# A recurrent state kept as diagonal blocks only, and one unit's transposes of r issued one addition later

## The chip, the cores and the metric

The kernel runs on one core of one Trainium2 chip. The metric is the device time of one execution in microseconds (us), lower is better. Every execution has such a time; a profiled one has, besides, a span from its first to its last instruction and a record of each instruction. The engines are called as in the profile: PE is TensorE (PEld its weight loads), DVE is VectorE, ACT is ScalarE, POOL is GpSimd, and SP is SyncE, which here issues the DMAs.

## What is computed

A linear attention with a decaying state (RWKV-6) is followed by a two-layer network with a SiLU between the layers. All is float32, with B = 4 batches, H = 8 heads, S = 768 time steps and D = 48 channels per head. The state of each batch and head is a 48x48 matrix, and in the reference it moves one step of time at a time:

```python
state = np.zeros((B, H, D, D))
for t in range(S):
    kt, vt, rt, wt = (k[:, :, t], v[:, :, t], r[:, :, t], w[:, :, t])
    cur = np.einsum('bhd,bhe->bhde', u[None] * kt, vt)
    y[:, :, t] = np.einsum('bhd,bhde->bhe', rt, state + cur)
    state = wt[:, :, :, None] * state + np.einsum('bhd,bhe->bhde', kt, vt)
x = y.transpose(0, 2, 1, 3).reshape(B * S, H * D)        # 3072 x 384
h = x @ w_in                                             # 384 x 2048
out = (h / (1 + np.exp(-h))) @ w_out                     # 2048 x 384
```

## The kernel before, in words

**Units.** Time is cut into six chunks of L = 128 steps, and the four batches into two pairs. That gives twelve units, numbered i = 0 to 11, with chunk n = i // 2. Units of one pair follow each other at a distance of two and hand on the state of that pair.

**Heads in pairs.** Eight heads of 48 channels lie as NP = 4 pairs p. The even head of a pair is in partitions 0 to 47 (e = 0), the odd one in partitions 64 to 111 (e = 1); PD = 64 is that distance. The state tile (line 289) holds for each batch and pair 128 columns: the even head's block stands in its rows at columns 0 to 47, the odd head's in its rows at columns 64 to 111. The two blocks are the diagonal of a 128x128 square, and the rest of it stays zero after `clear_state` (line 404).

**One unit.** The tokens of w, k and r come by DMA in 32x32 blocks (`load_blocks`) and are put channels-first by `turn` (line 374), two VectorE transposes of 128x512 for each of the three, one per batch. In the first two units `turn` uses TensorE instead. The products of w over 2, 4, ... 128 steps are made level by level on POOL (`product`, line 422). Keys are multiplied by them on POOL (`start_keys` at line 669, `grow_keys` at 645, `grow_own` at 654), and queries on VectorE (`grow_queries` at 627, `prepare` at 779). `burst` lets TensorE make the scores of two levels at once (line 703); `keep_level` puts them into the score tile. Then `y_state` (line 843) multiplies r by the state that the unit found, `y_values` (line 864) the scores by the values, and `update` makes the state for the pair's next unit: products k by v on TensorE (line 892), the old state times the decay of the whole chunk on POOL (line 897), and the sum of both on VectorE (line 906). `update` has the middle step only in chunks 1 to 4, that is in units 2 to 9, once per batch; the last chunk has no update.

**The network.** For each unit, `up` (line 1000) makes the hidden layer in eight steps, with the SiLU on ACT (line 1009). `quarter` (line 1066) makes the output in seven products of half-size blocks, in the manner of Strassen, from sums of the operands that VectorE makes beforehand (`sums`, line 1048; `weight_sums`, line 1040). The products take turns in two PSUM banks named p_o. Product 0's bank is emptied by a copy on ACT (line 1073), every later one's by one or two additions on VectorE (line 1075). So product 2 waits for the copy after product 0, and product 3 for the addition after product 1, which is the second.

**The order of work.** The order is written out by hand, and each engine executes its own instructions in that order. For unit 3 and later, `mix(i)` returns groups of steps of the scan, and the main loop puts steps of the network between them: the products of the output of unit i - 2 (`downs`), then the hidden layer of unit i - 1 (`ups`).

```python
for group, count in zip(groups, room):
    do(*group)
    for step in steps[:count]:
        do(*step)
    steps = steps[count:]
```

`room` for unit 3 begins 1, 1, 0, 2: after its first group comes product 0, after its second product 1, after its third nothing, after its fourth products 2 and 3. Unit 3 is the only one below NPAIR = 4 that goes through `mix`; later units have other groups, in which the turns of w and k are issued at the end of the unit before, behind `y_values`, and `update` comes after them; the turns of r and the first step of `grow_own` (lines 654 and 627) make the first group, and products 0 and 1 both follow it (their `room` begins 2, 1, 2, 2), so that the addition after product 1 stands behind them on VectorE.

**Queues.** Nearly all DMAs are issued by SP in the order of the program. A transpose on VectorE waits first for the DMA semaphores of its blocks.

Of the kernel before, what the change touches and what calls it, by code (L numbers as in the profile page):

```python
# [8 lines left out]
F32 = mybir.dt.float32  # L9
# [29 lines left out]
def kernel(  # L39
# [11 lines left out]
    nc = tc.nc  # L51

    B, H, S, D = r.shape
    DM, DF = moe_w_in.shape
    L = 128
    NL = 7
    NB = 2
    NP = H // 2
    PD = 64
# [14 lines left out]
    const = ctx.enter_context(tc.tile_pool(name="const", bufs=1))  # L74
# [9 lines left out]
    def bank(name, *dims):  # L84

        have = banks[name][turns_of[name] % 2][:]
        turns_of[name] += 1
        steps, n = [], 1
        for d in dims[::-1]:
            steps.insert(0, [n, d])  # L90
            n *= d
        return bass.AP(tensor=have.tensor, offset=have.offset, ap=[have.ap[0], *steps])
# [193 lines left out]
    make_identity(nc, ident)  # L286


    state = const.tile([128, B, NP, 2 * PD], F32, name="state")

    room = pt.tile([128, 4, DM // 2], F32, name="partial", bufs=1).rearrange("p x d -> p (x d)")
    spread = room[:, 0:4 * L].rearrange("p (s b t) -> p s b t", s=2, b=NB)
# [65 lines left out]
    tw, tr, tk, diag, kq, xt = {}, {}, {}, {}, {}, {}  # L358
# [472 lines left out]
    def values(i, b):  # L831
        return vq[i] if b == 1 else vt[i]

    def y_state(i):

        n, b0 = units[i]
        for e in range(2):
            p_yt[i, e] = bank("p_m", NP, L)
        for p in range(NP):
            for b in range(NB):  # L840
                for e in range(2):
                    rows = slice(PD * e, PD * e + D)
                    nc.tensor.matmul(y_place(i, e, p, b), lhsT=state[rows, b0 + b, p, rows],  # L843
                                     rhs=tr[i][rows, b * NP + p, :], start=(p < 2 and b == 0), stop=False)

        half = L // 2
        for p in range(NP):
            for b in range(NB):
                rows, at = slice(b * half, (b + 1) * half), (2 * p + b) * D
                nc.tensor.matmul(y_place(i, b, p, b)[:, 0:half], lhsT=whole[i][b][rows, at:at + D],  # L850
                                 rhs=score[rows, i % NSC, b, b * NP + p, 0:half], start=False, stop=False)

    def y_place(i, e, p, b):

        x = p % 2
        return p_yt[i, e][PD * x:PD * x + D, p // 2 * NB + b, :]
# [27 lines left out]
    def update(i, b):  # L884
        n, b0 = units[i]
        if n == S // L - 1:
            return
        if b == 0:
            p_kv[i] = bank("p_m" if i < NTOK else "p_sc", NB, NP, D)
        for p in range(NP):  # L890
            for e in range(2):
                nc.tensor.matmul(p_kv[i][PD * e:PD * e + D, b, p, :], lhsT=kq[i, b][:, p, PD * e:PD * e + D],
                                 rhs=values(i, b)[:, 2 * p + e, :], start=(b == 0 and p == 0),
                                 stop=(b == NB - 1 and p == NP - 1))
        new = state[:, b0 + b]
        if n > 0:
            nc.gpsimd.tensor_tensor(out=new, in0=new,
                                    in1=tw[i][NL][:, b * NP:(b + 1) * NP, :].to_broadcast([128, NP, 2 * PD]),
                                    op=ALU.mult)
        if b < NB - 1:  # L900
            return
        for e in range(2):
            rows, cols = slice(PD * e, PD * e + D), slice(PD * e, PD * e + D)
            new = state[rows, b0:b0 + NB, :, cols]
            if n > 0:
                nc.vector.tensor_tensor(out=new, in0=p_kv[i][rows], in1=new, op=ALU.add)
            else:
                (nc.scalar.copy if i == 0 else nc.vector.tensor_copy)(out=new, in_=p_kv[i][rows])
# [23 lines left out]
    def both(fn, i, *args):  # L932
        return [(fn, i, b, *args) for b in range(NB)]

    def block_loads(i, names="wkr"):
        return [(load_blocks, i, name, g) for name in names for g in range(4)]

    def mix(i):

        ahead = i + 1 < len(units)  # L940

        def at(now, *steps):
            return steps if now else ()

        def bonus_steps(j, *steps):
            return [(block_bonus, j, x) for x in steps]

        def sum_steps(j, *steps):
            return [(block_sum, j, x) for x in steps]

        def turns(j):
            return [*both(turn, j, "w"), (product, j, 0), *both(turn, j, "k")]

        def start(j):
            return [*[(product, j, l) for l in range(1, NL)], (grow_own, j, 1)]

        end = [[*at(ahead, *bonus_steps(i + 1, 0, 1, 2, 3))],
               [*at(i < len(units) - NB, (turn_apart, i), (turn_k, i)), (y_state, i), *both(y_values, i), *at(ahead, *turns(i + 1)),
                (sums, i - 1, FH // 2 - 2), *both(update, i), *at(not ahead, (move_x, i))]]
        if i < NPAIR:  # L960
            groups = [[*both(turn, i, "w"), (product, i, 0)],
                      [*both(turn, i, "k"), *both(turn, i, "r"), (odd_ones, i)], [(start_levels, i), (prepare_keys, i, 1)],
                      [(prepare, i, 1), *[(product, i, l) for l in range(1, NL)]],
                      [(burst, i, 1), (keep_level, i, 1)],
                      [(keep_level, i, 2), (go_on, i, 2)],
                      [(prepare, i, 3), (reverse_v, i), (bonus, i, 0)],
                      [(burst, i, 3), (keep_level, i, 3), (bonus_sum, i, 0), (bonus, i, 1), (bonus, i, 2)],
                      [(keep_level, i, 4), (go_on, i, 4), (bonus_sum, i, 1), (load_rk, i + 1), (load_u,)],
                      [(prepare, i, 5), (make_block_mask,), (bonus_spread, i), (bonus_write, i)],
                      [(burst, i, 5), (keep_level, i, 5), (keep_level, i, 6), (go_on, i, 6)], *end]  # L970
        else:
            groups = [[*both(turn, i, "r"), (grow_own, i, 0)], [*start(i), *sum_steps(i, 0, 1), *bonus_steps(i, 4, 5), (move_x, i - 1)],
                      [(odd_keys, i, 2), (grow_keys, i, 2, False), (grow_queries, i, 2), *sum_steps(i, 2)],
                      [(prepare, i, 3), *bonus_steps(i, 6, 7)],
                      [(burst, i, 3), (keep_level, i, 3), *sum_steps(i, 3, 4), (block_move, i), *at(ahead, (load_rk, i + 1))],
                      [(keep_level, i, 4), (go_on, i, 4)],
                      [(prepare, i, 5), (reverse_v, i)],
                      [(block_spread, i), (block_write, i)],
                      [(burst, i, 5), (keep_level, i, 5), (keep_level, i, 6), (go_on, i, 6)], *end]

        loads = [*at(i >= NPAIR and ahead, *block_loads(i + 1, "r")), *at(i + NSLOT < len(units), *block_loads(i + NSLOT, "wk"))]
        if i + 1 < len(units):
            loads.insert(len(loads) // 2, (load_values, i + 1))

        behind = groups[10 if i < NPAIR else 5 if i == NPAIR else 2:][:4 if i + NSLOT >= len(units) else None]
        for at, group in enumerate(behind):
            group += loads[at * len(loads) // len(behind):(at + 1) * len(loads) // len(behind)]
        return groups
# [127 lines left out]
    for l in range(1, NL):  # L1116
# [9 lines left out]


    others = {1: [(bonus_sum, 1, 0), (bonus_sum, 1, 1), (load_rk, 2), *blocks[8:12]], 2: [*both(update, 0)],
              3: [(bonus_spread, 1), (reverse_v, 1), (clear, 1), (load_values, 2)]}

# [19 lines left out]
    for m in range(6):  # L1150
# [8 lines left out]
    do((burst, 2, 5), (keep_level, 2, 5), (keep_level, 2, 6), (go_on, 2, 6), (bonus_write, 2), (up, 1, 6), (weight_sums, 1),  # L1159
       (load_values, 3), (turn_apart, 2), (turn_k, 2), (up, 1, 7), (weight_sums, 2), (sums, 1, 2))  # L1160
    do((sums, 1, 3), (y_state, 2), *both(y_values, 2), *both(update, 2),
       (move_x, 2),
       *blocks[7:])

    for i in range(3, len(units)):
        steps = downs(i - 2) + ups(i - 1)
        groups = mix(i)
        if i == NTOK + 1:
            groups[4].insert(1, (weight_sums, 3))
        room = (1, 1, 0, 2, 1, 1, 1, 1, 1, 2, 2, 1, 1) if i < NPAIR else (2, 1, 2, 2, 1, 1, 1, 2, 1, 1, 1)  # L1170
# [5 lines that stand above are left out]
# [32 lines left out]
```

## Time and profile before

| | |
|---|---|
| median of three runs | 605.8 us (603.47, 605.80, 605.83) |
| time of the profiled execution | 599.81 us |
| its span, first to last instruction | 598.0 us |
| busy: PE, PEld | 588.5, 528.1 us |
| busy: VectorE, POOL, ACT | 418.0, 363.3, 233.1 us |
| granted TensorE clock | 1.000 |
| moved by DMA | 53.42 MB, mean 89 GB/s |

A line of a group of instructions names the line of the kernel, the engine, the operation, the tile written and the tiles read, and the shapes (partitions x elements). For one tile's instructions the page gives the count, then the shortest, median and longest duration in ns and the first and last start. A line of the timeline begins with the start and the length in us, and merges neighbours of one form (x2); a bracket at its end gives how long the engine sat idle before and what released it. A line of the waits has the total in us, how often, and the longest. "Releasers" are inferred from semaphore events.

### The profile page before, as it was taken

What the parts mean: (1) busy time and instruction counts of PE and PEld (TensorE: products, weight loads), DVE (VectorE), ACT (ScalarE), POOL (GpSimd) and SP (SyncE); (2) the same over time, 40 slices, a digit from 0 to 9 for tenths busy, and PEclk for the clock granted to TensorE, in tenths of its full rate; (3) what the DMA queues carried; (4) which work ended last, traced back from release to release, by engine and by line L of the source; (5) the groups of instructions that cost most, each with busy time, mean ns of one, the idle gap of its engine ahead of it and who ended that gap; (6) DMA issues with size and microseconds to landing.
All of it is one profiled execution on the core that took longest, in us unless ns stands there. A gap on an engine that the chain in (4) does not pass through costs nothing.

```text
span 598.0 us, 14761 instructions
## 1 busy us (share of the span) xinstructions
PE 588.5 (98%) x5790; PEld 528.1 (88%) x5790; DVE 418.0 (70%) x709; ACT 233.1 (39%) x516; POOL 363.3 (61%) x414
## 2 busy tenths in 40 slices
PE   8999999999999999999999999999999999999997
PEld 7787876799899899898899899889889889889997
DVE  7879788798696695596696697687588587542041
ACT  6788884431530530440351361361351251250110
POOL 6998778247678668388578577577567667500000
PEclk9999999999999999999999999999999999999999
DMA  9956893443541543643643643643553531101000
GB/s 224 297 129 198 166 285 46 61 75 49 128 63 57 109 65 55 136 62 53 135 61 55 135 61 52 132 61 51 104 90 51 120 60 27 36 1 28 28 0 27
DMA packets 203078, 53.42 MB, mean 89 GB/s; under 512 B 186752, under 2 KB 194816, under 8 KB 203008
## 3 DMA queue, kind: packets, MB, share of 16 engines
q1 hardware_dynamic: 201424, 51.88, 42.6%
q8 instruction: 46, 0.75, 0.5%
q10 hardware_dynamic: 1584, 0.59, 0.5%
q14 instruction: 24, 0.20, 0.1%
HBM read 43.21 MB, written 5.24 MB: 81 GB/s over the span
## 4 chain that ended last, share of the span: by engine, by line
PE 77%; DVE 5%; DMA 5%; SPq 5%; POOL 3%; ACT 2%; issue 2%; DVEq 0%; POOLq 0%; ACTq 0%
PE p_h L1000 33%; PE p_o L1066 31%; SPq L123 3%; PE p_m L1022 3%; PE p_sc L703 2%; PE p_m L864 2%; PE p_m L843 2%; PE p_m L703 1%; DMA raw<-in_r_dram 1%; DMA tokens_rk<-in_k_dram 1%; DVE score L721 1%; DMA tokens_w<-in_w_dram 1%; POOL w_out_sb L255 1%; PE p_sc L819 1%; POOL tk L645 1%
## 5 line engine op out<-in xcount | busy, mean ns | idle before, releaser
L1000 PE MATMUL p_h<-xt,w_in_sb 128*128 128x256 f32 x1152 | 259.4, 382 | 0.9 <-POOL tk L669 0.7
L1000 PEld LDWEIGHTS p_h<-xt,w_in_sb 128*128 128x128 f32 x1152 | 215.7, 190 | 31.9 <-POOL tk L669 0.9
L1009 ACT ACTIVATE gt<-p_h 128x512 f32<-128x512 f32 x90 | 53.6, 596 | 171.4 <-PE p_h L1000 171.0
L645 POOL TENSOR_TENSOR tk<-tk,tw 128x256 f32<-128x256 f32 x128 | 93.6, 752 | 33.6 <-issue 20.7
L1066 PE MATMUL p_o<-own,temps 128*128 128x192 f32 x528 | 88.7, 327 | 1.6 <-DVE temps L1075 1.6
L507 POOL TENSOR_TENSOR ruk<-tokens_rk 128x768 f32<-128x768 f32 (+1 forms) x32 | 53.8, 1691 | 57.2 <-DMA tokens_rk<-in_k_dram 37.2
L1066 PEld LDWEIGHTS p_o<-own,temps 128*128 128x128 f32 x528 | 86.0, 190 | 2.6 <-DVE temps L1075 2.5
L1066 PE MATMUL p_o<-w_out_sb,gt 128*128 128x192 f32 x508 | 86.6, 327 | 0.0
L1066 PEld LDWEIGHTS p_o<-w_out_sb,gt 128*128 128x128 f32 x508 | 83.3, 190 | 1.0 <-DVE partial L1075 0.4
L1048 DVE TENSOR_TENSOR temps<-gt 128x256 f32<-128x256 f32 x84 | 53.2, 633 | 25.6 <-ACT gt L1009 25.3
L627 DVE TENSOR_TENSOR tr<-tr,tw 128x512 f32<-128x512 f32 x61 | 57.5, 942 | 16.0 <-PE p_m L703 12.5
L422 POOL TENSOR_TENSOR tw<-tw 128x256 f32<-128x256 f32 (+6 forms) x83 | 41.0, 494 | 36.4 <-DVE tw L374 32.5
L615 ACT COPY tk<-tk 128x256 f32<-128x256 f32 x52 | 20.9, 403 | 106.9 <-POOL tk L645 76.9
L721 DVE COPY_PREDICATED score<-mask,p_sc 128x512 f32<-128x512 int8 x42 | 31.2, 798 | 3.9 <-PE p_sc L703 3.7
L1048 DVE TENSOR_TENSOR temps<-temps,gt 128x256 f32<-128x256 f32 x43 | 32.3, 751 | 1.5
L1066 PE MATMUL p_o<-w_out_sb,temps 128*128 128x192 f32 x176 | 30.4, 326 | 0.0
L541 DVE TENSOR_REDUCE block_sums<-ruk 128x4 f32<-128x192 f32 (+1 forms) x48 | 24.2, 545 | 7.1 <-POOL ruk L507 7.1
L1066 PEld LDWEIGHTS p_o<-w_out_sb,temps 128*128 128x128 f32 x176 | 28.9, 190 | 0.0
L1075 DVE TENSOR_TENSOR temps<-p_o,partial 128x192 f32<-128x192 f32 x22 | 7.9, 358 | 29.8 <-PE p_o L1066 23.5
L869 ACT COPY yt<-p_m 48x512 f32<-48x512 f32 x40 | 23.2, 581 | 13.8 <-PE p_m L864 13.1
L1075 DVE TENSOR_TENSOR partial<-p_o,partial 128x192 f32<-128x192 f32 x33 | 11.7, 354 | 23.6 <-PE p_o L1066 23.6
L654 POOL TENSOR_TENSOR tk<-tk,tw 128x256 f32<-128x256 f32 x32 | 27.6, 883 | 0.0
(188 smaller groups left out, 811.2 us busy)
## 6 DMA issues: line engine op xcount, KB each, us to landing
w_out_sb<-in_moe_w_in_dram SPq DMA_DIRECT2D x6, 768.0 KB, 7.2
w_out_sb<-in_moe_w_out_dram SPq DMA_DIRECT2D x4, 768.0 KB, 6.3
own<-in_moe_w_out_dram SPq DMA_DIRECT2D x4, 768.0 KB, 5.7
tokens_rk<-in_r_dram SPq DMA_DIRECT2D x8, 384.0 KB, 4.3
tokens_rk<-in_k_dram SPq DMA_DIRECT2D x8, 384.0 KB, 5.3
tokens_w<-in_w_dram SPq DMA_DIRECT2D x8, 384.0 KB, 6.3
xt<-yt SPq DMA_DIRECT2D x60, 48.0 KB, 1.9
raw<-in_w_dram SPq DMA_DIRECT2D x80, 32.0 KB, 2.1
```

Of the source, the lines that this page charges most:

```text
L422: engine.tensor_tensor(out=up, in0=t[:, :, 0::2], in1=t[:, :, 1::2], op=ALU.mult)
L507: mul = lambda out, one, two: nc.gpsimd.tensor_tensor(out=out, in0=one, in1=two, op=ALU.mult)
L541: add = lambda out, have: nc.vector.tensor_reduce(out=out, in_=have, axis=mybir.AxisListType.X, op=ALU.add)
L627: nc.vector.tensor_tensor(out=odd, in0=odd, in1=tw[i][l][:, :, 0::2][:, :, :, None].to_broadcast([128, Q, L >> (l + 1), c]), op=ALU.mult)
L645: nc.gpsimd.tensor_tensor(out=out, in0=have, in1=odd_products(i, l, b, *blocks), op=ALU.mult)
L654: nc.gpsimd.tensor_tensor(out=have, in0=have, in1=odd_products(i, l, b, [2, NP * ni]), op=ALU.mult)
L721: nc.vector.copy_predicated(out=dst, mask=masks[l][:, :, None].to_broadcast([128, NB, NP, ni, c]), data=sc[e].rearrange("p (b q) (i c) -> ...
L869: nc.scalar.copy(out=yt[i][PD * e:PD * e + D, x::2, :, :], in_=p_yt[i, e][PD * x:PD * x + D].rearrange("p (q b) t -> p q b t", b=NB))
L1000: nc.tensor.matmul(p_h[:, a, :], lhsT=w_in_sb[:, c, f * 128:(f + 1) * 128], rhs=xt[i][:, c, :], start=(c == 0), stop=(c == KC - 1))
L1009: nc.scalar.activation(out=gt[i, m], in_=p_h, func=AF.Silu)
L1048: nc.vector.tensor_tensor(out=out, in0=one, in1=two, op=op)
L1066: nc.tensor.matmul(p, lhsT=left(f), rhs=right[:, f, :], start=(f == 0), stop=(f == FH - 1))
```

## The change

The state tile loses the columns that were always zero: each batch and pair now has 48 columns, and both heads' blocks start at column 0, each in its own partitions. `y_state`, the product with the decay and the sum in `update` use the new columns. In the groups of unit 3, the turns of r leave the second group, where they stood behind the turns of k, and become the first steps of the third. Between these two groups lies product 1 with its addition.

```diff
-    state = const.tile([128, B, NP, 2 * PD], F32, name="state")
+    state = const.tile([128, B, NP, D], F32, name="state")
...
-                    nc.tensor.matmul(y_place(i, e, p, b), lhsT=state[rows, b0 + b, p, rows],
+                    nc.tensor.matmul(y_place(i, e, p, b), lhsT=state[rows, b0 + b, p, :],
                                      rhs=tr[i][rows, b * NP + p, :], start=(p < 2 and b == 0), stop=False)
...
             nc.gpsimd.tensor_tensor(out=new, in0=new,
-                                    in1=tw[i][NL][:, b * NP:(b + 1) * NP, :].to_broadcast([128, NP, 2 * PD]),
+                                    in1=tw[i][NL][:, b * NP:(b + 1) * NP, :].to_broadcast([128, NP, D]),
                                     op=ALU.mult)
...
-            rows, cols = slice(PD * e, PD * e + D), slice(PD * e, PD * e + D)
-            new = state[rows, b0:b0 + NB, :, cols]
+            rows = slice(PD * e, PD * e + D)
+            new = state[rows, b0:b0 + NB]
...
             groups = [[*both(turn, i, "w"), (product, i, 0)],
-                      [*both(turn, i, "k"), *both(turn, i, "r"), (odd_ones, i)], [(start_levels, i), (prepare_keys, i, 1)],
+                      [*both(turn, i, "k"), (odd_ones, i)], [*both(turn, i, "r"), (start_levels, i), (prepare_keys, i, 1)],
```

## The prediction

> **What bounds the kernel now.** I read the page first (busy shares), then TensorE's waits in order of length, then the state tile's own instructions, and last the order of time around the waits.
>
> ```profile
> PE 588.5 (98%) x5790; PEld 528.1 (88%) x5790; DVE 418.0 (70%) x709; ACT 233.1 (39%) x516; POOL 363.3 (61%) x414
> ```
>
> TensorE (PE) is busy for all but 9.5 us of 598.0. The table by stretches puts 3.1 us of those before 36 us and 1.6 us between 36 and 121.5 us, where nothing of the change but one memset lies. After that 4.8 remain, in which the waits over 0.1 us are:
>
> ```profile
> PE p_o L1066 <- DVE temps L1075: 1.6, 3, 1.1
> ```
>
> Three waits, 1.6 us together (the other 3.2 are small gaps without a releaser), all of a quarter product (line 1066) for the addition (line 1075) that empties the bank of the second product. The waits by window put them at 132 us (0.37), 180 us (0.17) and 272 us (1.10). I call them S3, S4 and S6, by the unit whose r is being turned. Now the state's own work:
>
> ```profile
> L843 PEld LDWEIGHTS p_m<-tr,state x320: 116/120/120, 120.5 to 532.8; 48*48 48x48 f32 x160
> L843 PE MATMUL p_m<-tr,state x320: 269/269/308, 120.5 to 533.0; 48*48 48x128 f32 x160
> L897 POOL TENSOR_TENSOR state<-state,tw x16: 1215/1265/1927, 121.7 to 447.2; 128x512 f32<-128x512 f32 x16
> L404 POOL MEMSET state<- x1: 1816/1816/1816, 9.4 to 9.4; 128x2048 f32 x1
> ```
>
> Sixteen GpSimd (POOL) products of 512 elements. Unit 3's place in time, VectorE (DVE), then TensorE:
>
> ```profile
> 128.24 1.30 DVE L374 STREAM_TRANSPOSE tw<-raw 128x512 f32<-128x512 f32 x2
> 129.47 1.26 DVE L374 STREAM_TRANSPOSE tk<-raw 128x512 f32<-128x512 f32 x2
> 130.66 1.26 DVE L374 STREAM_TRANSPOSE tr<-raw 128x512 f32<-128x512 f32 x2
> 131.95 0.36 DVE L1075 TENSOR_TENSOR temps<-p_o,partial 128x192 f32<-128x192 f32 x1
> ```
>
> ```profile
> 129.23 2.76 PE L1066 MATMUL p_o<-own,temps 128*128 128x192 f32 x16
> 132.36 2.87 PE L1066 MATMUL p_o<-own,temps 128*128 128x192 f32 x16 [0.37 <-DVE temps L1075]
> ```
>
> The second product was done near 129.3; its addition waits behind three pairs of transposes, and the fourth product cannot start at 131.99. At S6 the same addition ends at 272.99, TensorE was ready at 271.94 (DVE, POOL, PE):
>
> ```profile
> 264.08 1.15 DVE L1048 TENSOR_TENSOR temps<-temps,gt 128x256 f32<-128x256 f32 x1
> 265.15 1.26 DVE L1048 TENSOR_TENSOR temps<-gt 128x256 f32<-128x256 f32 x1
> ...
> 272.63 0.36 DVE L1075 TENSOR_TENSOR temps<-p_o,partial 128x192 f32<-128x192 f32 x1
> ```
>
> ```profile
> 263.63 2.50 POOL L897 TENSOR_TENSOR state<-state,tw 128x512 f32<-128x512 f32 x2
> 266.09 2.01 POOL L654 TENSOR_TENSOR tk<-tk,tw 128x256 f32<-128x256 f32 x2
> ```
>
> ```profile
> 273.04 3.19 PE L1066 MATMUL p_o<-own,temps 128*128 128x192 f32 x18 [1.10 <-DVE temps L1075]
> ```
>
> VectorE has no gap from 250.57 to 272.99, so whatever shortens its work there shortens S6.
>
> **What the skill says.** (1) "SBUF — State Buffer", Who interferes with whom: a VectorE instruction with two SBUF inputs and a GpSimd one that reads SBUF exclude each other for a whole instruction; with one input it doesn't contend. The trace agrees: line 1048 takes 0.42 us alone, 1.15 and 1.26 beside line 897; transposes take 0.66 to 0.71 always. (2) "GPSIMD Engine Reference", 3.1: about 2.6 cycles per element of a two-input operation. At its 1.2 GHz, 320 elements fewer would be 0.69 us (an estimate). The trace's rows of 512 and 192 elements differ by 1.04 − 0.59 = 0.45; I use the rows. (3) "TensorE: Matmul & The Clock Gate", Step-by-step: a weight load's time goes by columns. The trace has 120 ns for 48, 190 for 128. The state's loads keep 48.
>
> **The change, part by part.** *Smaller memset*: line 404 falls from 2048 to 768 elements; the row of line 303 (768 elements) says 0.73, so 1.1 us less. Cover: POOL then sits idle 2.65 us until VectorE's product at 13.7. Nothing; without cover 1.1 (the upper bound); never a loss.
>
> *State product on POOL*: 512 to 192 elements, sixteen times. No row has this shape with this broadcast; bounds are 0.59 (192 elements alone, line 507) and 0.80, which adds the 0.21 by which line 897 beside VectorE (1.25) exceeds 512 elements alone (1.04). I take 0.80: 0.45 less each, 7 us of POOL in all, none of it on TensorE's path directly (it waits for no line 897). What counts is the lock: two VectorE instructions end about 0.3 us after each of the two POOL products, so VectorE moves ahead by 2 × 0.45 = 0.9 us per unit. Bounds: 0 (the next POOL products, line 654, move up and block instead) to 2 × (1.25 − 0.59) = 1.3.
>
> *Packed state in VectorE's addition (line 906)*: 384 elements on 48 partitions before and after, 0.55 us, one input in PSUM: nothing; ±0.02 at most, as the state's two strides already vary by that (539 to 561 ns). *Loads of line 843*: same partitions and 48 columns: nothing; the other end is a rival below.
>
> *Turns of r of unit 3 moved*: two transposes and their semaphore waits go behind one addition on VectorE; nothing on SP's, POOL's or ACT's queue passes anything. The addition could then start at 130.70 and end by 131.1, before 131.99: S3's 0.37 gone, and transposes end at 132.3, 0.35 later. Queued behind the addition, which waits for the second product, are r's turns, line 627 and line 779, and for these the first burst of unit 3 (135.16) waits. VectorE cannot lose by it: were it early, the addition would wait until 129.4, still before 130.66. With the lock relief (two instructions of line 1048 at 122.6 and 123.9 took 1.27 and 1.15) k is turned by about 130.0 and the addition done by 130.4. But what is late next: the burst's loads began 0.2 us after their predecessors, released by line 645 on POOL, whose start follows w's and k's turns. With the move alone TensorE would come to the burst at 134.9 and wait there up to 0.3; since relief moves VectorE's turns and thus POOL by 0.7, I count the whole 0.37.
>
> *S4*: VectorE's addition comes 0.9 earlier against a lateness of 0.17 plus the 0.37 that TensorE is now ahead: gone, 0.17. *S6*: 1.10 − 0.90 leaves 0.20: 0.90 gained, if the chain before it (lines 560 to 577: a DMA out and back, then VectorE) moves up with TensorE. If SP's queue holds it, S4's and S3's gain is waited for again and the total is 0.90.
>
> Sum: 0.37 + 0.17 + 0.90 = **1.44 us**; bounds 0.07 and 1.64. The profiled execution has a span of 598.0 and a time of 599.81; it should become 596.6 and 598.4. The runs shown have a median of 605.8, 6.0 above the profiled one, for which the profile gives no reason; I subtract the same: 605.8 − 1.44 = **604.4**.
>
> **Rivals.** *The waits only move* (TensorE meets the bursts or the chain through DMA early): for it, S3's next releaser, line 645, is 0.2 us behind; against, POOL and VectorE both get shorter. Gain 0.1 to 0.5: 605.5. *The move does nothing of its own*: with relief alone the old order ends the addition at 132.3 − 0.7 = 131.6, before 131.99; then same time, 604.4, the packing the cause; it is part of the forecast. *More than the waits*: the memset and all relief on the path, 1.64 + 1.1, and half of the 3.2 of small gaps: 4.3, so 601.5; against, POOL's idle time behind the memset, and gaps without a releaser. *Slower*: packed blocks load worse. Line 843's 32 products come every 33 ns in ten units, on TensorE's path, since loads of two row halves overlap; if halves that now start at the same column offset stop overlapping like that and 120 ns went to the 190 of a full load, a stretch of 1.06 us grows by 0.62, ten times 6.2: 605.8 − 1.4 + 6.2 = 610.6. It decides from 1.44 / 320 = 4.5 ns per product. Against: partitions, columns and order stay; only addresses change.
>
> **Chances.** Forecast 0.66 (with the move redundant or not), waits only move 0.20, more 0.05, slower 0.09. Half a per cent, 3.0 us, is about what a measurement can tell from no change. The first three fall inside it unless the runs scatter against it: those of before spread 2.3 us below their median. So faster by over 0.5% has 0.13 (the 0.05 and an eighth of the forecast), slower 0.06 (two thirds of that rival), the same 0.81. The range goes down by 2.3 from 604.2 (all three waits gone) to 601.9, and up to 607.0, which takes in no gain and the slower rival up to 8 ns per product.
>
> **What would show it.** Right: line 897 at 0.6 to 0.8 us; line 1048 beside it at 0.7 to 0.8; in unit 3 the addition ahead of r's turns; TensorE's wait for line 1075 at 0.2 or less in all; y from the state (line 843) still 1.06 us. Wrong: a new wait of TensorE for line 645 or 627 at a burst, or S6 still over 0.7 (the lock given to line 654, or SP's chain late), or 843 longer.

## The result, and the profile after

Over 22 executions each, the kernel before has a median of 600.76 us and the changed one 598.99 us. The ratio is 0.9961, with a 95% interval of 0.9943 to 0.9979: faster by 0.4%, that is by 2.3 us, between 1.3 and 3.4; the medians lie 1.8 us apart. The profiled execution of the changed kernel has a span of 597.3 us. The three executions of before that stood behind the prediction (603.47, 605.80, 605.83) lie at the upper end of the 22, of which the lowest is 599.18. The predicted 604.4 missed for that reason and the range with it; the step from one kernel to the other, 1.44 us, lies inside the interval.

The page of the changed kernel, busy shares:

```profile
PE 587.5 (98%) x5790; PEld 527.8 (88%) x5790; DVE 411.6 (69%) x709; ACT 232.7 (39%) x516; POOL 351.5 (59%) x414
```

POOL works 11.8 us less and VectorE 6.4 less, though VectorE has the same instructions. The state tile's own instructions (shortest, median, longest in ns):

```profile
L843 PE MATMUL p_m<-tr,state x320: 269/269/307, 121.4 to 532.3; 48*48 48x128 f32 x160
L897 POOL TENSOR_TENSOR state<-state,tw x16: 679/734/1736, 122.6 to 445.7; 128x192 f32<-128x192 f32 x16
L906 DVE TENSOR_TENSOR state<-p_sc,state x16: 540/551/561, 127.0 to 448.1; 48x384 f32<-48x384 f32 x16
L404 POOL MEMSET state<- x1: 742/742/742, 9.3 to 9.3; 128x768 f32 x1
```

All products on POOL but the first are down from between 1.22 and 1.32 us to between 0.68 and 0.79. The products by the state on TensorE are as they were (269 ns each). TensorE's waits over 0.1 us after 122 us are down to one, a new one:

```profile
PE p_h L1000 <- ACT gt L1009: 0.6, 1, 0.6
```

In this profile nothing waits for line 1075 any more. Unit 3 on VectorE, then quarter products 2 and 3 on TensorE:

```profile
129.38 1.26 DVE L374 STREAM_TRANSPOSE tk<-raw 128x512 f32<-128x512 f32 x2
130.67 0.36 DVE L1075 TENSOR_TENSOR temps<-p_o,partial 128x192 f32<-128x192 f32 x1
130.94 1.29 DVE L374 STREAM_TRANSPOSE tr<-raw 128x512 f32<-128x512 f32 x2
```

```profile
130.20 5.36 PE L1066 MATMUL p_o<-own,temps 128*128 128x192 f32 x32
```

The addition stands ahead of r's turns, and products 2 and 3 are one run of 32 matmuls without a bracket. The place at 272 us, VectorE and then POOL:

```profile
264.19 0.61 DVE L1048 TENSOR_TENSOR temps<-temps,gt 128x256 f32<-128x256 f32 x1
264.73 0.72 DVE L1048 TENSOR_TENSOR temps<-gt 128x256 f32<-128x256 f32 x1
265.37 1.06 DVE L1048 TENSOR_TENSOR temps<-gt,temps 128x256 f32<-128x256 f32 x1
...
269.26 1.29 DVE L374 STREAM_TRANSPOSE tr<-raw 128x512 f32<-128x512 f32 x2
```

```profile
263.74 1.43 POOL L897 TENSOR_TENSOR state<-state,tw 128x192 f32<-128x192 f32 x2
265.13 2.01 POOL L654 TENSOR_TENSOR tk<-tk,tw 128x256 f32<-128x256 f32 x2
```

The first two of these instructions of line 1048 take 0.61 and 0.72 us where they took 1.15 and 1.26; the third still stands beside line 654. I use two measures in what follows. **Gap k to r**: from the end of k's turns to the start of r's turns of the same unit on VectorE. It was 270.23 − 263.74 = 6.49 us and is 269.26 − 263.85 = 5.41. It repeats to 0.02 us over units 4 to 10 of each of the two kernels. **Lengths**: the time from one unit's first weight load of line 843 on TensorE ("first 843") to the next unit's, and from unit 2's to the end ("stretch"), which leaves out the start-up. The column 2→3 holds the waits in unit 3, 3→4 that at 180 us, 5→6 that at 272 us. Lengths from unit 6 on are the same in all runs within 0.01 us, but for one run, where two neighbours trade 1.07.

| profile (us) | first 843 | 2→3 | 3→4 | 4→5 | 5→6 | stretch | gap k to r |
|---|---|---|---|---|---|---|---|
| before | 120.47 | 45.17 | 45.80 | 45.78 | 47.33 | 477.56 | 6.48 |
| after | 121.43 | 45.54 | 45.18 | 45.93 | 45.78 | 475.90 | 5.42 |
| before_again | 121.56 | 46.22 | 45.93 | 45.83 | 46.86 | 478.31 | 6.48 |
| after_again | 121.00 | 45.44 | 45.18 | 45.96 | 46.22 | 476.27 | 5.41 |
| move_only | 121.10 | 46.09 | 45.93 | 46.13 | 46.36 | 478.00 | 6.48 |
| pack_only | 120.66 | 44.97 | 45.18 | 45.78 | 45.78 | 475.17 | 5.42 |
| wide_product | 120.73 | 46.07 | 45.98 | 45.78 | 46.35 | 477.65 | 6.48 |
| ballast_read | 120.83 | 45.19 | 45.55 | 45.82 | 46.50 | 476.54 | 5.96 to 6.20 |
| ballast_write | 123.49 | 45.28 | 45.18 | 49.86 | 45.78 | 479.57 | 5.69 to 5.89 |
| ballast_write2 | 122.75 | 45.83 | 45.18 | 45.88 | 45.78 | 476.14 | 5.69 to 5.89 |
| diag_on_act | 121.14 | 46.01 | 45.18 | 45.78 | 45.78 | 476.23 | 5.41, once 5.95 |
| loads_later | 123.33 | 44.49 | 51.04 | 45.78 | 45.78 | 480.56 | 5.42, once 7.05 |
| moves_first | 120.82 | 44.78 | 45.18 | 45.78 | 45.78 | 474.99 | 5.42 |

### The profile page after: what moved, and what is told of

Its sections match the earlier page's. It is cut to its first block, busy times and chain, and to the rows that moved or that the text cites. A ratio compares the mean times of both kernels' runs of the same rounds, so it can differ in the third digit from the quotient of the medians.

```text
span 597.3 us, 14760 instructions
## 1 busy us (share of the span) xinstructions
PE 587.5 (98%) x5790; PEld 527.8 (88%) x5790; DVE 411.6 (69%) x709; ACT 232.7 (39%) x516; POOL 351.5 (59%) x414
## 4 chain that ended last, share of the span: by engine, by line
PE 82%; DVE 5%; POOL 4%; ACT 2%; SPq 2%; DMA 2%; issue 2%; POOLq 0%; DVEq 0%; ACTq 0%
PE p_h L1000 35%; PE p_o L1066 34%; PE p_m L1022 3%; PE p_m L864 2%; PE p_sc L703 2%; PE p_m L843 2%; SPq L123 2%; PE p_m L703 1%; DVE score L721 1%; POOL w_out_sb L255 1%; PE p_sc L892 1%; PE p_sc L819 1%; DMA own<-in_moe_w_out_dram 1%; DMA raw<-in_r_dram 1%; DVE score L604 1%
## 5 line engine op out<-in xcount | busy, mean ns | idle before, releaser
L645 POOL TENSOR_TENSOR tk<-tk,tw 128x256 f32<-128x256 f32 x128 | 93.9, 755 | 35.4 <-issue 21.0
L507 POOL TENSOR_TENSOR ruk<-tokens_rk 128x768 f32<-128x768 f32 (+1 forms) x32 | 51.4, 1616 | 64.4 <-DMA tokens_rk<-in_k_dram 34.6
L1048 DVE TENSOR_TENSOR temps<-gt 128x256 f32<-128x256 f32 x84 | 50.3, 599 | 25.7 <-ACT gt L1009 25.3
L627 DVE TENSOR_TENSOR tr<-tr,tw 128x512 f32<-128x512 f32 x61 | 54.1, 887 | 14.7 <-PE p_m L703 11.2
L1048 DVE TENSOR_TENSOR temps<-temps,gt 128x256 f32<-128x256 f32 x43 | 29.1, 677 | 1.5
L703 PEld LDWEIGHTS p_sc<-tr,tk 48*64 48x64 f32 x960 | 17.3, 134 | 12.1 <-issue 7.7
```

Source lines behind the costliest of these rows:

```text
L507: mul = lambda out, one, two: nc.gpsimd.tensor_tensor(out=out, in0=one, in1=two, op=ALU.mult)
L627: nc.vector.tensor_tensor(out=odd, in0=odd, in1=tw[i][l][:, :, 0::2][:, :, :, None].to_broadcast([128, Q, L >> (l + 1), c]), op=ALU.mult)
L645: nc.gpsimd.tensor_tensor(out=out, in0=have, in1=odd_products(i, l, b, *blocks), op=ALU.mult)
L703: nc.tensor.matmul(to, lhsT=tk[i][rows, X[l % 2] + p, x * 64:(x + 1) * 64], rhs=have, start=True, stop=True)
L1048: nc.vector.tensor_tensor(out=out, in0=one, in1=two, op=op)
```

## The experiments

My theory was that the shorter product on POOL frees VectorE's second input earlier, that this alone takes away all three waits, and that the move of r adds nothing to it. The rivals: the move does the work in unit 3; the packed layout helps by itself; the gain is start-up chance.

**Each part alone.** The kernel with the move and the wide state:

```diff
-                      [*both(turn, i, "k"), *both(turn, i, "r"), (odd_ones, i)], [(start_levels, i), (prepare_keys, i, 1)],
+                      [*both(turn, i, "k"), (odd_ones, i)], [*both(turn, i, "r"), (start_levels, i), (prepare_keys, i, 1)],
```

> The state as before, only the turns of r in unit 3 moved. Stretch used as a measure: from the first product of r by the state (line 843 of unit 2) to the end, 477.5 us before and 475.9 after the change. Theory (lock): the wait of 0.37 at product 3 of unit 3 goes, but line 645 on POOL is not earlier, so the first burst of unit 3 takes back up to 0.3 of it; the waits at 180 us (0.17 or a little more) and at 272 us (1.1) stay. Stretch 477.2 to 477.5, ratio of times 0.999 to 1.000. Rival (the move does the work, and the later waits follow from unit 3): at least half of the gain, stretch 476.7 or less.

Measured: ratio 1.0011 (0.9991 to 1.0030), stretch 478.00. TensorE after the addition was moved:

```profile
129.87 5.36 PE L1066 MATMUL p_o<-own,temps 128*128 128x192 f32 x32
135.16 0.70 PE L703 MATMUL p_sc<-tr,tk 48*64 48x64 f32 x32
136.31 0.69 PE L703 MATMUL p_m<-tr,tk 48*64 48x64 f32 x32 [0.45 <-POOL tk L645]
```

Products 2 and 3 run through, and then the second half of the burst waits 0.45 us for POOL's keys. The wait for line 1075 became a wait for line 645. The stretch is longer than expected (477.2 to 477.5), because the wait for ACT in unit 3 is in it too, of which below.

The packed state with r's turns in their old place is the changed kernel with that line reversed:

> The state packed, the turns of r where they were. Theory (lock): line 1048 beside the state product takes 0.6 and 0.7 instead of 1.15 and 1.26 us, the addition after product 1 of unit 3 ends near 131.6 or just in time for product 3, and the waits at 180 and 272 us go: stretch from the first line 843 to the end 476.2 or less, nearly all of the gain, ratio of times 0.996 to 0.998. Rival (the move is half of it): a wait of 0.2 us or more for line 1075 in unit 3, stretch near 476.7.

Measured: ratio 0.9972 (0.9957 to 0.9987), stretch 475.17, gap 5.42. VectorE and TensorE:

```profile
129.78 1.26 DVE L374 STREAM_TRANSPOSE tr<-raw 128x512 f32<-128x512 f32 x2
131.07 0.36 DVE L1075 TENSOR_TENSOR temps<-p_o,partial 128x192 f32<-128x192 f32 x1
```

```profile
129.43 5.36 PE L1066 MATMUL p_o<-own,temps 128*128 128x192 f32 x32
```

The addition still follows r's turns, and ends at 131.43, before product 2 does. All three waits are gone. The move is worth nothing that these profiles show, and the intervals of the times (around 0.9972 and 0.9961) overlap over most of their length.

**The same kernels once more**, to see what chance does:

> The kernel before, unchanged, to see what one more profiled execution gives. Theory: the start of the first line 843 (120.5 in the first profile of before, 121.4 after the change) varies by about 1 us with the landing of the weights' DMAs, whatever the kernel; the three waits for line 1075 appear again at 132, 180 and 272 us with 1.6 us together, give or take 0.3; ratio of times 0.998 to 1.002. Rival (the waits are chance too): their sum under 1.0 or over 2.2.

> The changed kernel, unchanged, once more. Theory: no wait for line 1075 over 0.1 us; stretch from the first line 843 to the end 475.5 to 476.3, whatever the start of that stretch is; ratio of times 0.994 to 0.998. In unit 3 a wait of TensorE for ACT (line 1009), 0.6 us in the first profile, appears again if SP's queue is behind it, smaller if the start of the stretch is earlier. Rival (the gain of the first comparison is mostly start-up chance): stretch 477 or more.

Measured: 0.9991 (0.9976 to 1.0005) and 0.9966 (0.9951 to 0.9981). The gain repeats. In before_again the waits are these:

```profile
PE p_o L1066 <- DVE temps L1075: 1.3, 3, 0.6
PE p_h L1000 <- ACT gt L1009: 0.6, 1, 0.6
```

The three waits for line 1075 are there again, the one at 272 us only about half as long, and the wait for ACT that looked new in the changed kernel is there too. So it is no effect of the change. In after_again the matmul row shows no wait for line 1075, but 0.44 us stay in 5→6, and the weight loads show 0.3 of it as a wait for line 1075. So the change does not always take the wait at 272 us away whole.

**Layout or length.** Both blocks at column 0 and the move, but tile and product 128 columns wide:

```diff
-    state = const.tile([128, B, NP, D], F32, name="state")
+    state = const.tile([128, B, NP, 2 * PD], F32, name="state")
...
-                    nc.tensor.matmul(y_place(i, e, p, b), lhsT=state[rows, b0 + b, p, :],
+                    nc.tensor.matmul(y_place(i, e, p, b), lhsT=state[rows, b0 + b, p, 0:D],
...
-                                    in1=tw[i][NL][:, b * NP:(b + 1) * NP, :].to_broadcast([128, NP, D]),
+                                    in1=tw[i][NL][:, b * NP:(b + 1) * NP, :].to_broadcast([128, NP, 2 * PD]),
...
-            new = state[rows, b0:b0 + NB]
+            new = state[rows, b0:b0 + NB, :, 0:D]
```

> The changed kernel, both heads' blocks at column 0 and the turns of r moved, but the tile and the product on POOL (and the memset) again 128 columns wide, so that only the layout and the move of the change are left. Theory (the shorter product is what helps): line 897 at 1.2 to 1.3 us, line 1048 beside it at 1.15 and 1.26, the wait for line 1075 at 272 us returns with 0.6 to 1.1; ratio of times to before 0.999 to 1.001. Rival (the layout of loads and additions helps): ratio 0.996 to 0.998 and no such wait.

Measured: ratio 1.0010 (0.9994 to 1.0026), gap 6.48 as before, stretch 477.65. TensorE's waits after 122 us:

```profile
PE p_h L1000 <- ACT gt L1009: 0.5, 1, 0.5
PE p_m L703 <- POOL tk L645: 0.4, 1, 0.4
PE p_o L1066 <- DVE temps L1075: 0.3, 1, 0.3
```

It behaves like move_only, down to the wait for line 645 (0.45 us in both). The wait at 272 us returns with 0.3 us on this row and 0.57 in the length 5→6, less than the 0.6 to 1.1 expected, and little more than the 0.44 of after_again: the column 5→6 alone would not separate the two. Three other figures do. The gap k to r is 6.48 and not 5.42; 3→4 is 45.80 to 45.98 in the four profiles with a wide product, and 45.18 in all with a short one but ballast_read and loads_later; and the intervals of the times of wide_product on one side and of after_again and pack_only on the other do not meet. The layout alone gives nothing. This kernel has the wide memset as well, so it doesn't separate that from the product; what shows the memset to be worth nothing is POOL's idle time behind it, 2.65 us before and 3.72 after the change, until the same product of VectorE (line 422) in both.

**The lock, measured by itself.** Behind each short product one more instruction on POOL, a ballast that nobody needs, once reading SBUF and once only writing it:

```diff
+    idle = const.tile([128, 640], F32, name="idle")
+    nc.gpsimd.memset(idle, 0.0)
...
+        if n > 0:
+            nc.gpsimd.tensor_tensor(out=idle[:, 0:160], in0=idle[:, 0:160], in1=idle[:, 160:320], op=ALU.add)
```

In the other kernel the last line is `nc.gpsimd.memset(idle[:, 0:560], 0.0)`.

> The changed kernel with one more POOL instruction behind each of the sixteen state products: an addition of 160 elements that reads a scratch tile, about 0.55 us, which nobody needs. POOL then works about as long per state product as before the change. Theory (lock): line 1048 beside it is held up again, VectorE loses 0.7 to 1.2 us per unit, and the wait for line 1075 at 272 us returns with 0.7 to 1.2 us, the one at 180 us with 0.1 to 0.3; stretch from the first line 843 to the end 476.7 to 477.3. Rival (the packed layout itself is what helps): no wait returns, stretch 475.9.

> The same ballast in time, but a memset of 560 elements, about 0.55 us, which reads nothing. Theory (a VectorE instruction with two SBUF inputs shuts out only a POOL instruction that reads SBUF): line 1048 runs through at 0.42 beside it, VectorE loses under 0.3 us, no wait for line 1075 over 0.2; stretch 475.8 to 476.2. Rival (it is POOL's own lateness that matters, by the keys of line 654 that come after): the same loss as with the reading ballast, stretch 476.7 to 477.3.

Measured: 0.9982 (0.9967 to 0.9997) with the reading ballast, 0.9975 (0.9958 to 0.9991) with the memset. The first profile of the memset kernel is of an execution of 604.85 us, against a median of 599.51; in it TensorE waited 2.2 us for xt, the network's input, so that its stretch of 479.57 says nothing of the ballast. For a second one:

> The kernel with the memset ballast once more, for a profile in which no other disturbance stands (in the first, TensorE waited 2.2 us for xt). Theory: no wait for line 1075 over 0.2, stretch from the first product by the state to the end 475.2 to 476.3. Rival: the wait for xt or for line 1075 comes with the ballast, stretch over 476.7.

VectorE of that second profile, then POOL (line 1048 is 1052 in this kernel, 897 is 899, 654 is 656):

```profile
265.93 0.61 DVE L1052 TENSOR_TENSOR temps<-temps,gt 128x256 f32<-128x256 f32 x1
266.46 0.41 DVE L1052 TENSOR_TENSOR temps<-gt 128x256 f32<-128x256 f32 x1
266.80 0.72 DVE L1052 TENSOR_TENSOR temps<-gt,temps 128x256 f32<-128x256 f32 x1
```

```profile
265.48 0.78 POOL L899 TENSOR_TENSOR state<-state,tw 128x192 f32<-128x192 f32 x1
266.21 0.56 POOL L903 MEMSET idle<- 128x560 f32 x1
266.73 0.51 POOL L899 TENSOR_TENSOR state<-state,tw 128x192 f32<-128x192 f32 x1
```

The middle one lies beside the memset and takes 0.41 us; the other two lie beside the products and take 0.61 and 0.72. The second product takes 0.51 us, where in the changed kernel it takes 0.68. Here the addition that the first product held up is over (266.54) before the second product starts (266.73); there that addition runs until 264.80, and the second product has started at 264.49. That POOL is held up in its turn is my reading of these times. In the reading kernel the same place reads, VectorE and then POOL:

```profile
263.81 0.61 DVE L1052 TENSOR_TENSOR temps<-temps,gt 128x256 f32<-128x256 f32 x1
264.34 0.74 DVE L1052 TENSOR_TENSOR temps<-gt 128x256 f32<-128x256 f32 x1
265.01 0.72 DVE L1052 TENSOR_TENSOR temps<-gt,temps 128x256 f32<-128x256 f32 x1
```

```profile
264.11 0.70 POOL L903 TENSOR_TENSOR idle<-idle 128x160 f32<-128x160 f32 x1
264.76 0.69 POOL L899 TENSOR_TENSOR state<-state,tw 128x192 f32<-128x192 f32 x1
```

All three are held up. The gap k to r grows from 5.42 by 0.54 to 0.78 us with the reading ballast, and by 0.27 to 0.47 with the memset, where POOL's later products come later and meet other instructions of line 1048. I had expected 0.7 to 1.2 and under 0.3: the direction is right, the contrast smaller. The reading ballast brings back 0.37 of 3→4 and 0.72 of 5→6, the memset neither; but TensorE's matmul row shows no wait over 0.1 us for the addition of line 1075 with either, where I had expected 0.7 to 1.2 at 272 us, and the stretch of 476.54 stays just under the 476.7 expected. The two ballasts are not quite alike in length (0.70 and 0.56 us), and the times don't tell them apart. What separates reading from writing is the single instruction, 0.74 us beside the one and 0.41 beside the other. That agrees with what the Trainium skill says on "SBUF — State Buffer", Who interferes with whom: two SBUF inputs on VectorE contend with a GpSimd instruction that reads SBUF, not with one that only writes it. That page gives the length of the lock, a whole instruction, beside another mode of VectorE; here the addition held up ends 0.27 to 0.28 us after the product beside it, whether that has 512 or 192 elements.

**What stands in unit 3.** In eight of the thirteen profiles TensorE waits there for line 1009 on ACT. In the changed kernel, ACT, TensorE and SP's queue:

```profile
155.41 0.20 ACT L595 COPY both_b<-diag 128x16 f32<-128x16 f32 x1 [2.09 <-DMA diag<-own_sums]
156.64 0.84 ACT L597 COPY both_b<-diag 32x16 f32<-32x16 f32 x4 [1.03 <-DMA diag<-own_sums]
157.39 1.06 ACT L1009 ACTIVATE gt<-p_h 128x512 f32<-128x512 f32 x2
```

```profile
158.03 8.39 PE L1000 MATMUL p_h<-xt,w_in_sb 128*128 128x256 f32 x36 [0.63 <-ACT gt L1009]
```

```profile
142.72 9.22 SPq L123 DMA_DIRECT2D raw<-in_r_dram  x16
152.04 0.40 SPq L1079 DMA_DIRECT2D out_dram<-ob  x1
152.54 0.38 SPq L1079 DMA_DIRECT2D out_dram<-temps  x1
153.01 2.45 SPq L467 DMA_DIRECT2D diag<-own_sums  x4
```

ACT's SiLU stands behind copies of the bonus (the term with u in the reference), these wait for the DMAs of line 467, and these stand on SP behind sixteen loads of r for unit 4. Three kernels try the order of DMAs on top of the change. First the loads behind:

```diff
-       *blocks[7:])
+       *blocks[7:8])
...
-                      [(keep_level, i, 4), (go_on, i, 4), (bonus_sum, i, 1), (load_rk, i + 1), (load_u,)],
+                      [(keep_level, i, 4), (go_on, i, 4), (bonus_sum, i, 1), (load_rk, i + 1), (load_u,), *block_loads(i + 1, "r")],
```

> The changed kernel with the sixteen DMAs of unit 4's r issued behind unit 3's bonus DMAs and row loads instead of ahead of them on SP. Theory (in unit 3 SP's queue takes back what was gained): the DMAs of line 467 start 5 us or more earlier, ACT's copies behind them too, the wait of TensorE for line 1009 near 157 us is gone and the other one near 165 too: stretch from the first line 843 to the end 474.9 to 475.6, 0.3 to 1.0 less than after the change; ratio to before 0.993 to 0.997. Rival (that wait belongs to ACT's own order, or the loads of r are then late): no less than 475.9.

Measured: ratio 1.0036 (1.0021 to 1.0051), slower. The wait for line 1009 is gone (2→3 is 44.49), though counted from the first 843 the DMAs of line 467 start only 1.2 us earlier, not 5; and 5.9 us are lost one unit later, on TensorE:

```profile
194.65 0.67 PE L1000 MATMUL p_h<-xt,w_in_sb 128*128 128x256 f32 x2 [1.23 <-DMA xt<-yt]
196.26 0.67 PE L1000 MATMUL p_h<-xt,w_in_sb 128*128 128x256 f32 x2 [0.94 <-DMA xt<-yt]
198.42 14.01 PE L1000 MATMUL p_h<-xt,w_in_sb 128*128 128x256 f32 x56 [1.49 <-DMA xt<-yt]
```

The network's input for unit 3 arrives late: line 928 begins on SP at 190.18 instead of 181.85 (1.9 us of that are start-up, as the first 843 shows), since SP issues other loads without a break up to it. Right after the last wait the granted clock is 0.51 for 3.4 us (198.8 to 202.2; 1.00 before and behind), and 56 matmuls take 14.01 us. In the first memset profile 60 take 13.22 at a clock of 1.00, so 56 would take 12.3: the low clock costs some 1.7 us (an estimate from these figures), the waits 3.7. My expectation looked at one end of the queue only. Then the four DMAs issued by ACT:

```diff
-                nc.sync.dma_start(out=diag[i][b][s::2], in_=own_sums[b * L // 2:(b + 1) * L // 2, s])
+                (nc.sync if i == NTOK else nc.scalar).dma_start(out=diag[i][b][s::2], in_=own_sums[b * L // 2:(b + 1) * L // 2, s])
```

> The changed kernel with the four DMAs of line 467 of unit 3 issued by ACT instead of SP, so that they don't stand behind the loads of r and the stores of the output. Theory (SP's queue makes unit 3's bonus late): the copies of line 595 start 1 us or more earlier than in the changed kernel relative to TensorE, the wait of TensorE for line 1009 near 157 us (0.6 us) is gone, the stretch 475.0 to 475.6; the gain in time, 0.3 to 0.7 us against the changed kernel, is hardly to be told from none. Rival (ACT's issuing costs it as much): the wait stays, 475.9 or more.

Measured: ratio 0.9980 (0.9967 to 0.9993), the wait longer. ACT, then TensorE:

```profile
151.51 2.47 ACTq L467 DMA_DIRECT2D diag<-own_sums  x4
154.03 0.60 ACT L1009 ACTIVATE gt<-p_h 128x512 f32<-128x512 f32 x1 [4.86 <-DMA diag<-own_sums]
```

```profile
154.68 2.86 PE L1000 MATMUL p_h<-xt,w_in_sb 128*128 128x256 f32 x12 [1.25 <-ACT gt L1009]
```

Issuing four DMAs holds ACT for 2.47 us, and the SiLU waits for that instead, as the rival had it. Last, the loads at the end of a unit's order put behind the DMAs to xt:

```diff
+    later = {}
...
-                      (move_x, i - 1)],
+                      (move_x, i - 1), *later.pop(i, [])],
...
-            group += loads[at * len(loads) // len(behind):(at + 1) * len(loads) // len(behind)]
+            part = loads[at * len(loads) // len(behind):(at + 1) * len(loads) // len(behind)]
+            if group is groups[-1] and ahead:
+                later[i + 1] = [x for x in part if x[0] is load_blocks]
+                part = [x for x in part if x[0] is not load_blocks]
+            group += part
```

> The changed kernel with the block loads that stand at the end of each unit's order put behind the next step's DMAs of line 928 (which bring y to the network's input xt) instead of ahead of them. Nothing is left out. Theory (SP's queue is what the slow executions wait in: xt arrives late and TensorE waits 2 us): line 928 starts 5 us or more earlier after units 3 to 9, no execution of over 602 us, and the median 0.3 to 1.0 us lower than the changed kernel's: ratio 0.994 to 0.996. Rival (the loads that are now late are what the turns wait for): slower, a wait of VectorE at line 374.

Measured: 0.9975 (0.9963 to 0.9987), median 598.91, highest 601.96. Line 928 begins at 173.91 after unit 3, 7.9 us earlier than in the changed kernel, and no turn waits. But the ratio is not the expected 0.994 to 0.996, and the times can't be told from the changed kernel's (0.9966, with an interval that overlaps). Its stretch of 474.99 is the shortest of all, but 0.76 of the 0.91 us to 475.90 lie in 2→3, ahead of the first load that this kernel moves, and so are chance. So no version here is shown to beat the changed kernel.

## Why the prediction was right and wrong

- **The level was wrong.** The failing step is "I subtract the same: 605.8 − 1.44". It took the distance of 6.0 us between the profiled execution and the median of three as something that both kernels have. Over 22 executions that distance is 0.95 us (600.76 against 599.81). All sets of executions put before at 600.76 (22), 600.82 (48), 601.31 (45) and 600.37 us (51). The sum against the profiled execution gave 598.4; measured were 598.99. The low end of the range was cut from the same three values.
- **Where the gain is: right.** S3 and S4 went, and S6 wholly or in good part, by the shorter product on POOL, with the memset (0.74 us, foreseen 0.73), line 906 and line 843 worth nothing. The slower rival did not come: line 843's matmuls take 269 ns as before, and the 32 of a unit start within 0.86 us as before (28 ns apart; the prediction's 33 is 1.06 us by 32). Wide_product excludes a gain from layout.
- **The relief of VectorE was mis-sized a little.** It was put at 2 × 0.45 = 0.90 us per unit. The gap k to r says 1.06. Line 897 beside VectorE takes 0.73 us, the mean of its two usual values, not 0.80.
- **The waits were read too small.** The sum used 0.37, 0.17 and 1.10 from TensorE's matmul row. In time, S3 cost about 0.63 (the changed kernel is 0.96 us late at unit 2's first line 843 and 0.33 at the burst, which begins at 135.16 before and 135.49 after), S4 0.62 (45.80 to 45.18), S6 1.55 (47.33 to 45.78), together 2.8. The row of the weight loads had it nearly right:

```profile
PEld p_o L1066 <- DVE temps L1075: 2.5, 3, 1.4
```

  The Trainium skill says on "Perfetto Trace Analysis", Identifying the Most-Contended Engine, that the busy share of the matmul row is no good measure of how close a kernel is to the roofline, and that of the weight loads is one; it says nothing of single waits. Here the two rows differ by 0.9 us over three waits, and the lengths side with the weight loads.
- **What is late next: right.** The move alone was said to meet line 645 with up to 0.3 us; it met it with 0.45. That the packing makes the move redundant was said too, and pack_only shows it.
- **Not foreseen:** the wait of unit 3 for ACT. Of the 2.8 us that the first pair of profiles gained in S3, S4 and S6, about 1.04 were given back there (0.28 late at 145 us, 1.32 at 166) and 0.15 in 4→5, which leaves about what the stretch shows, 477.56 − 475.90 = 1.66. That the sum of 1.44 came close to this is in part luck: waits read too small on one side, a loss not foreseen on the other. As before and before_again show, the same kernel twice (2→3 of 45.17 and 46.22), these parts come and go. S6 varies as well (0.57 to 1.55 among the four profiles with a wide product).

What stays open is why three executions of before in a row were near 605. One execution of such a length was profiled, the 604.85 of the memset kernel. Against the profile of the changed kernel (599.11) its first 843 comes 2.06 us later, and its stretch is 3.67 longer; that makes 604.84. The loss in the stretch lies in 4→5 (49.86 against 45.93): TensorE waits 2.2 us for xt, and from 243.8 to 247.2 the granted clock is 0.50. For 144 executions of before (the sets of 48, 45 and 51) the mean clock is on record: it is 0.997 or less in 15, all of which took 601.89 us or more, and in 8 of the 12 that took over 603. So a stretch of low clock goes with many of the long executions. That the three were of this kind is not shown.

## What to carry to other kernels

When an engine that is not the bottleneck is shortened, look at which instructions of its neighbour stand beside it: here TensorE waited for none of the 16 products, yet shortening them freed 1.06 us of VectorE per unit, and VectorE had held up TensorE. Price a stall of TensorE from the weight loads' row and from the distance between two fixed points, not from the matmul row. And predict the step and the level apart: the median of three lay 5.0 us above that of 22, one profiled execution of before 0.95 below it, another (601.74) 0.98 above. Only many executions say where the level is.

## What the runs showed of the hardware

- An addition of two SBUF inputs on VectorE takes 0.42 us alone, 1.15 and 1.26 beside a product of 512 elements on POOL, 0.61 and 0.72 beside one of 192. POOL seems to pay too: the product of 512 took 1.22 to 1.32 us beside these additions, another of 512 alone (line 422) 1.04; the short one 0.68 to 0.79, and 0.51 where the addition held up before it was over when it started.
- SP's queue is a resource: sixteen small loads held it for 9.2 us in unit 3, and moved to a later place, still ahead of line 928, they cost TensorE 3.7 us of waiting.
- In the two profiles in which TensorE waited for xt, a wait of 2.2 us and waits of 3.7 us in three parts, the granted clock was about 0.5 for 3.4 us right afterwards.
- Issuing a DMA costs the issuing engine: 2.47 us of ACT for four.
